# Modulation as columns, and the two gate rows multiplied in the prologue of a DiT block

## The chip, the cores and the metric

The kernel runs on one core of a Trainium2 chip. The metric is the device time in microseconds (us) of one execution. The kernel before took 2003.08 us as the median of three runs, from 2000.74 to 2003.76 us. The execution that was profiled is another one, of 2006.96 us, of which 2005.2 us lie between the first and the last instruction.

A word on names. TensorE is PE in the rows of the profile, and its weight loads are PEld. VectorE is DVE, ScalarE is ACT, GpSimd is POOL, and SyncE, which here only issues DMAs, is SP. A fp32 matmul with a full 128x128 stationary operand stands in the profile as two weight loads and two matmul records. I call one such pair a pass.

## The reference, cut to what matters

```python
x = A_x                                     # 1 x 2048 x 512, fp32
mod = silu(c) @ w_mod                       # c: 1 x 512, w_mod: 512 x 3072 -> six rows of 512
sa, ca, ga, sb, cb, gb = mod.reshape(6, 512)
h = layernorm(x) * (1 + ca) + sa
x = x + ga * attention(h, wqkv, wo)         # 32 heads of 16, softmax over 2048 keys
h = layernorm(x) * (1 + cb) + sb
x = x + gb * mixer(h, w1, w2, w3, w4)       # two token-shift / MLP stages with layernorm and gelu
```

The change is all in `mod`. Six slices of `silu(c) @ w_mod` are needed. `sa` and `ca` are used where features lie on partitions, so there each of them is a set of four columns of 128 values. `ga`, `gb`, `sb` and `cb` are used where features lie along the free axis, so each is a row of 512, the same in all 128 partitions.

## The kernel before, in words

The program has three stages. In the **prologue** x arrives in four chunks of 512 rows (`load_x`). Each chunk is normalised (`ln1`), transposed on TensorE into features on partitions (`ln1_T`, line 585), modulated with the columns `modcol`, and split into a high and a low part (`hT`). The high part is made on ScalarE (lines 590, 611, 594). The whole value comes from ScalarE or, for two of four feature blocks, from VectorE (line 597). The low part is made on GpSimd for three of four blocks (line 603). From `hT` come the first keys and queries (`qk_first`). Every product is three matmuls, high by high, high by low and low by high (lines 339, 341, 343). In **attention**, 64 units of (512 query rows, one pair of heads) follow each other. A unit has 32 score blocks on TensorE (line 1009), as many blocks for the row maximum of the unit that comes one and a half units later (line 993, reduced on VectorE in line 989), their exponentials on ScalarE (line 1005), the low half of the probabilities on GpSimd (line 1057, or ScalarE in line 127), and the product with v (lines 1080 and 1083). At its end ScalarE copies the accumulator out (line 1101), once per unit. Between the blocks of attention, TensorE is given **fill**: in the first quarter, units 0 to 15, that is the rest of k, q and v, and the modulation rows. In later quarters it is the mixer of the quarter before. The **end** is the mixer of the last quarter.

The order on each engine is fixed when the program is built. A planner (class `Sched`) keeps a made-up clock per engine. Generators are asked for their next piece of TensorE work whenever there is credit (700 ns of fill per step in the first quarter, 800 to 900 at its start). Follow-up work on the other engines is held in chains and put where the planner's clock has room. What the planner writes is executed strictly in order on every engine, whatever the true times are. All DMAs are issued by SP in the planner's order. Each of them waits for the DMA that stands eight before it.

The modulation before goes as follows.

- `load_wm(k)` loads four tiles `wm` of 128 x 1024, the first two slices of `w_mod`, two of them ahead of the first chunk of x and two behind it.
- `mod_cols` multiplies them with a broadcast `sil` as the stationary operand (line 550), eight fp32 matmuls of 512 columns. The results are rows, equal in all partitions. VectorE takes columns out of them with the identity (line 555), eight pairs of instructions.
- `mod_rows` makes the four rows within attention, from when the key group 1 is done, by `mod_gen`: for each row four chunks of 128 columns. Each chunk has one DMA of 256 KB into a staging tile `wst`, four fp32 matmuls of 128 columns (line 633) and one VectorE copy (line 637). The order is `garow`, `gbrow`, `cbrow`, and `sbrow` last, since `garow` and `sbrow` share a tile.
- `pieces_load` splits the weights of the later stages in the background. It waits for `garow` ahead of `wo` and for `gbrow` ahead of `w4`.

The first weights of v (`v_weights`) need a bound `vb`: four matmuls (line 784), then a chain on VectorE (lines 790 to 798), then a scaling on GpSimd (line 804) and a split (lines 441 and 439). With that done, the v matmuls start.

Of the kernel before, what the change touches and what calls it, by code (L numbers as in the profile page):

```python
# [310 lines left out]
def kernel(ctx, tc, A_x, A_wqkv, A_wo, B_w1, B_w2, B_w3, B_w4, c, w_mod, out):  # L311
# [23 lines left out]
    def mark(key):  # L335
        return None, 0, lambda: done.add(key)
# [9 lines left out]
    def nsq(n):  # L346
        return 0.4405 * n + 6
# [65 lines left out]
    dve.tensor_scalar(ident, iot, 0.0, None, op0=OP.is_equal)  # L413
# [95 lines left out]
    dve.tensor_tensor(sil, sil, cc, op=OP.mult)  # L509
    silb = [sil[:, k:k + 1].to_broadcast([P, P]) for k in range(KT)]  # L510
# [33 lines left out]
    def mod_cols():  # L544
        scr0 = sp.tile([P, P], F32, name="scr0")
        bs = [dbank("mr") for _ in range(2)]
        for k in range(KT):
            yield lambda: sch.now() >= arr["wm", k]
            for j in range(2):
                te.matmul(bs[j], silb[k], wm[k][:, j * D:(j + 1) * D], start=(k == 0), stop=(k == KT - 1))  # L550
                yield 4 * nsq(CH)
        for j, b in enumerate(bs):

            def diag(i, j=j, b=b):
                dve.tensor_tensor_reduce(out=scr0, in0=b[:, i * P:(i + 1) * P], in1=ident, scale=1.0, scalar=float(j),
                                         op0=OP.mult, op1=OP.add, accum_out=modcol[:, 4 * j + i:4 * j + i + 1])
                if i == 3:
                    sch.free(b)
            sch.chain(*[("D", 210, partial(diag, i)) for i in range(4)], mark(("mod", j)))

# [275 lines left out]
    def mod_rows():  # L836
        yield lambda: ("kq", 1) in done
        yield from mod_gen((2, garow, 0.0))
        done.add("garow")
        yield from mod_gen((5, gbrow, 0.0))  # L840
        done.add("gbrow")
        yield from mod_gen((4, cbrow, 1.0))
        yield lambda: all(("wo", 2 * i + c) in done for i in order["wo"] for c in range(2))
        yield from mod_gen((3, sbrow, 0.0))
        done.add("mods")
# [74 lines left out]
    for g in (mod_cols(), bounds(), ln1_T(), qk_first(hi, lo), weights_gen(), qkv_gen(0), qkv_gen(1, 2, 3, 4, 5, 6)):  # L920
        sch.add(g)
    drain(("q", 0, 0))
    for ci in range(NC):
        drain(("k", 0, ci))
        load_first(ci)
    while sch.owner or sch.back:
        sch.step()
        sch.room()
# [755 lines left out]
```

## Time and profile before

| | |
|---|---|
| median of three runs | 2003.08 us (2000.74 to 2003.76) |
| the profiled execution | 2006.96 us, span 2005.2 us |
| busy share of the span | PE 96%, DVE 82%, ACT 73%, POOL 84% |
| granted TensorE clock, mean | 0.986 |
| units 0 to 15, from the first copy of an accumulator to the seventeenth | 134.8 to 579.6 us |
| busy in that stretch (444.8 us) | PE 424.3, DVE 380.3, ACT 357.3, POOL 406.4 us |

A busy PE is not a PE at its peak: the ends of matmuls are modelled, and a record of 390 ns is followed by the next one 230 ns later. So the share of PE says little here, and starts of rows that follow each other say more. In the rows that are quoted, a bracket at the end of a row of the timeline tells how long the engine was idle before it and what ended that.

### The profile page before, as it was taken

The page shows a single profiled execution, that of the slowest core. Times are in us where ns is not written, and L with a number is a line of the kernel's source. Part 1 is how long each engine was busy: PE and PEld are TensorE (multiplying, and loading weights), DVE is VectorE, ACT ScalarE, POOL GpSimd, SP SyncE. Part 2 cuts the span into 40 slices and gives each one's busy share as a digit, 9 for nine tenths or more (in the row PEclk, how much of TensorE's full clock was granted, in tenths as well). Part 3 has the DMA queues.
Part 4 walks back from the last instruction along what each step waited for, and adds up shares of the span by engine and source line. Part 5 has one row for each costly group of instructions (what it writes and reads, how often), then busy time and mean ns, then how long its engine had stood idle before and what let it go on. Part 6 is the DMA issues. An engine that isn't in the chain of part 4 may idle for free.

```text
span 2005.2 us, 42362 instructions
## 1 busy us (share of the span) xinstructions
PE 1920.3 (96%) x14464; PEld 1146.1 (57%) x14464; DVE 1653.2 (82%) x3025; ACT 1466.3 (73%) x3072; POOL 1682.4 (84%) x1612
## 2 busy tenths in 40 slices
PE   6989999999999999999999999999999999999899
PEld 4655555555455555555455555555545555555798
DVE  7888988888898988888989888898898889892643
ACT  5375898777878887786878677787787778786443
POOL 6386999999989998888999988898898989897532
PEclk8999999999999999999999999999999999999999
DMA  5676677876543434344433333344433343333432
GB/s 186 197 205 198 199 228 218 266 231 205 174 152 111 118 132 136 97 145 138 133 106 115 107 96 111 108 136 136 152 104 97 111 136 114 111 116 111 180 146 90
DMA packets 232352, 293.24 MB, mean 146 GB/s; under 512 B 125876, under 2 KB 177076, under 8 KB 215848
## 3 DMA queue, kind: packets, MB, share of 16 engines
q1 hardware_dynamic: 232136, 290.53, 46.2%
q8 instruction: 115, 1.88, 0.4%
q14 instruction: 101, 0.83, 0.1%
HBM read 225.81 MB, written 62.91 MB: 144 GB/s over the span
## 4 chain that ended last, share of the span: by engine, by line
PE 65%; DVE 16%; ACT 8%; POOL 5%; issue 3%; DMA 2%; SPq 1%; POOLq 0%; DVEq 0%; ACTq 0%
PE mb L993 14%; DVE mx L989 9%; PE sc L1009 9%; PE pv L1083 9%; PE w L339 7%; PE w L341 6%; PE w L343 6%; PE pv L1080 4%; ACT pt L1005 4%; POOL pt L1057 3%; DVE xs L1406 1%; DVE sq L1403 1%; PE ot L1112 1%; PE mr L633 1%; SPq L106 1%
## 5 line engine op out<-in xcount | busy, mean ns | idle before, releaser
L1057 POOL TENSOR_SCALAR pt<-pt 128x1024 f16<-128x1024 uint16 x993 | 1318.9, 1367 | 120.1 <-ACT pt L1005 114.2
L989 DVE TENSOR_REDUCE mx<-mb 128x1 f32<-128x512 f32 x2048 | 1280.8, 682 | 79.2 <-PE mb L993 49.9
L1005 ACT ACTIVATE pt<-sc 128x512 int32<-128x512 f32 x2048 | 1088.6, 607 | 274.5 <-PE mb L993 214.0
L993 PE MATMUL mb<-kst,qtl 64*128 64x512 f32 x2048 | 753.2, 454 | 50.3 <-ACT pt L1005 16.5
L1009 PE MATMUL sc<-qtl,kst 64*128 64x512 f32 x2048 | 716.5, 444 | 3.8 <-DVE mx L989 1.1
L993 PEld LDWEIGHTS mb<-kst,qtl 64*128 64x128 f32 x2048 | 348.1, 193 | 257.3 <-DVE mx L989 90.1
L1009 PEld LDWEIGHTS sc<-qtl,kst 64*128 64x128 f32 x2048 | 335.8, 186 | 154.7 <-DVE mx L989 50.3
L1083 PE MATMUL pv<-pt,vst 128*32 128x512 f16 x4096 | 358.6, 397 | 0.0
L1080 PE MATMUL pv<-pt,vst 128*25 128x512 f16 (+1 forms) x2048 | 211.7, 394 | 2.0 <-POOL pt L1057 2.0
L1083 PEld LDWEIGHTS <-vst 128*32 128x32 bf16 x4096 | 91.3, 95 | 166.5 <-issue 107.9
L1413 POOL TENSOR_TENSOR g<-xs,g 128x256 fp32r<-128x256 f32 (+2 forms) x144 | 103.2, 718 | 89.1 <-ACT g L1412 86.9
L339 PE MATMUL w<-A,wr 128*128 128x256 f32 (+2 forms) x576 | 175.9, 305 | 0.8 <-ACT A L333 0.6
L341 PE MATMUL w<-A,wr 128*128 128x256 f32 (+2 forms) x576 | 170.8, 296 | 0.7 <-DVE A L329 0.7
L343 PE MATMUL w<-A,wr 128*128 128x256 f32 (+2 forms) x576 | 168.0, 292 | 0.0
L339 PEld LDWEIGHTS w<-A,wr 128*128 128x128 f32 x576 | 110.2, 191 | 35.8 <-ACT pt L1005 12.0
L339 PE MATMUL w<-wr,g 128*128 128x512 f32 x288 | 119.1, 414 | 0.6 <-ACT g L1412 0.6
L341 PEld LDWEIGHTS w<-A,wr 128*128 128x128 f32 x576 | 110.4, 192 | 13.5 <-issue 12.2
L343 PE MATMUL w<-wr,g 128*128 128x512 f32 x288 | 115.2, 400 | 0.9 <-POOL g L1413 0.9
L1520 DVE TENSOR_TENSOR x<-x,w 128x512 f32<-128x512 f32 x64 | 43.9, 686 | 85.5 <-PE w L343 85.2
L343 PEld LDWEIGHTS w<-A,wr 128*128 128x128 f32 x576 | 110.7, 192 | 5.6 <-issue 5.6
L341 PE MATMUL w<-wr,g 128*128 128x512 f32 x288 | 113.7, 395 | 0.0
L1409 ACT ACTIVATE sq<-w 128x256 f32<-128x256 f32 (+2 forms) x144 | 55.9, 388 | 72.7 <-PE w L343 69.7
(147 smaller groups left out, 2083.5 us busy)
## 6 DMA issues: line engine op xcount, KB each, us to landing
wr<-Ws SPq DMA_DIRECT2D x80, 1024.0 KB
kst<-Ks SPq DMA_DIRECT2D x189, 256.0 KB
vst<-Vs SPq DMA_DIRECT2D x252, 192.0 KB
qtl<-Qs SPq DMA_DIRECT2D x192, 64.0 KB
Vs<-vt SPq DMA_DIRECT2D x32, 384.0 KB
Ws<-wq SPq DMA_DIRECT2D x40, 256.0 KB
Ws<-wst SPq DMA_DIRECT2D x40, 256.0 KB
wst<-in_B_w_dram SPq DMA_DIRECT2D x36, 256.0 KB
```

Source lines behind the costliest of these rows:

```text
L339: te.matmul(o, lh, rh, start=first, stop=False)
L341: te.matmul(o, lh, rl, start=False, stop=False)
L343: te.matmul(o, ll, rh, start=False, stop=last)
L989: end = sch.crit("D", 605, e + PX, lambda: dve.reduce_max(mxs[u][:, j, g, c:c + 1], b, axis=AX.X))
L993: return ready, lambda: te.matmul(b, lhs, kst[u % 3][r, c * CH:(c + 1) * CH], start=True, stop=True), after
L1005: ea = sch.crit("A", 480, e + PX, lambda: act.activation(pt[s][:, j], b, AF.Exp))
L1009: return ready, lambda: te.matmul(b, kst[u % 3][r, kt * P:(kt + 1) * P], qst[u][r], start=True, stop=True), after
L1057: e_low[s] = XP["G"] + sch.crit("G", 1345, ready, lambda: pool.tensor_scalar(o, i, 0.5, 1.0, op0=OP.mult, op1=OP.mult))
L1080: te.matmul(acc[r:r + n, :], v[:, (kt + i) % 4, c - n:c].bitcast(F16), pt[s + i].bitcast(F16)[:, j, 0::2], start=False, stop=kt == NKT - 2 ...
L1083: te.matmul(acc[r:r + 32, :], v[:, kt % 4, r:r + 32], pt[s].bitcast(F16)[:, j, 1::2], start=kt == 0, stop=False, skip_group_check=True)
L1409: sch.chain(("A", cA(n), lambda: act.activation(sq, b, AF.Square)), ("D", cD(n), cube), ("A", cA(n), lambda: act.activation(sq, sq, AF.Tan ...
L1413: ("G", cG(n), lambda: pool.tensor_tensor(lo, xs, hi, op=OP.subtract)), (None, 0, end), bank=b)
```

## The change

The two slices of the columns are now multiplied the other way round. The tile of `w_mod` is the stationary operand and one column of `sil` is moved, 32 fp32 matmuls with one column each (new line 571), all into eight columns of one PSUM bank. VectorE then needs two small instructions (new line 578) in place of eight pairs. The identity is made after `sil`.

As soon as tile k of `wm` has been used, `load_wm2(k)` refills its buffer with slices 2 and 5 of `w_mod`, two DMAs of 256 KB. `mod_gates` multiplies them as rows: eight fp32 matmuls of 512 columns (new line 557), and ScalarE copies them into `garow` and `gbrow` (new line 561). `mod_rows` keeps only `cbrow` and `sbrow`. The loop at the end of the prologue waits in the planner for both gate rows.

```diff
--- before.py
+++ after.py
@@ -410,7 +410,6 @@
     psd["d"] = pp
     iot = sp.tile([P, P], I32, name="iot")
     pool.iota(iot, pattern=[[1, P]], base=0, channel_multiplier=-1)
-    dve.tensor_scalar(ident, iot, 0.0, None, op0=OP.is_equal)
 
     hT = [qp.tile([P, KT, 2, CH], F32R, name=f"hT{i}") for i in range(NC)]
     garow = sbrow
@@ -507,6 +506,7 @@
     dve.tensor_scalar(sil, sil, 1.0, None, op0=OP.add)
     dve.reciprocal(sil, sil)
     dve.tensor_tensor(sil, sil, cc, op=OP.mult)
+    dve.tensor_scalar(ident, iot, 0.0, None, op0=OP.is_equal)
     silb = [sil[:, k:k + 1].to_broadcast([P, P]) for k in range(KT)]
 
 
@@ -541,23 +541,44 @@
         sch.chain(*[("D", 670, partial(stats, t)) for t in range(TPC)], ("G", 1300, rstd), (None, 0, applies),
                   prio=2 * (ci > 1), ready=arr["x", ci])
 
-    def mod_cols():
-        scr0 = sp.tile([P, P], F32, name="scr0")
+    wm2 = {}
+
+    def load_wm2(k):
+        wm2[k] = sp.tile([P, 2 * D], F32, name="wm", tag="wm", bufs=KT)
+        for j in range(2):
+            arr["wm2", k] = sch.dma(dma.dma_start, wm2[k][:, j * D:(j + 1) * D], w_mod[k * P:(k + 1) * P, (2 + 3 * j) * D:(3 + 3 * j) * D])
+
+    def mod_gates():
+        yield lambda: len(wm2) == KT and sch.room(2)
         bs = [dbank("mr") for _ in range(2)]
         for k in range(KT):
+            yield lambda: sch.now() >= arr["wm2", k]
+            for j in range(2):
+                te.matmul(bs[j], silb[k], wm2[k][:, j * D:(j + 1) * D], start=(k == 0), stop=(k == KT - 1))
+                yield 4 * nsq(CH)
+
+        def out(d, b):
+            act.activation(d, b, AF.Copy)
+            sch.free(b)
+        for b, d, key in zip(bs, (garow, gbrow), ("garow", "gbrow")):
+            sch.chain(("A", cA(), partial(out, d, b)), mark(key), bank=b)
+
+    def mod_cols():
+        b = dbank("mr")[:, :8]
+        for k in range(KT):
             yield lambda: sch.now() >= arr["wm", k]
-            for j in range(2):
-                te.matmul(bs[j], silb[k], wm[k][:, j * D:(j + 1) * D], start=(k == 0), stop=(k == KT - 1))
-                yield 4 * nsq(CH)
-        for j, b in enumerate(bs):
-
-            def diag(i, j=j, b=b):
-                dve.tensor_tensor_reduce(out=scr0, in0=b[:, i * P:(i + 1) * P], in1=ident, scale=1.0, scalar=float(j),
-                                         op0=OP.mult, op1=OP.add, accum_out=modcol[:, 4 * j + i:4 * j + i + 1])
-                if i == 3:
-                    sch.free(b)
-            sch.chain(*[("D", 210, partial(diag, i)) for i in range(4)], mark(("mod", j)))
-
+            for i in range(8):
+                te.matmul(b[:, i:i + 1], wm[k][:, i * P:(i + 1) * P], sil[:, k:k + 1], start=(k == 0), stop=(k == KT - 1),
+                          skip_group_check=True)
+                yield 150
+            load_wm2(k)
+
+        def cols(j):
+            c = slice(4 * j, 4 * j + 4)
+            dve.tensor_scalar(modcol[:, c], b[:, c], float(j), None, op0=OP.add)
+            if j:
+                sch.free(b)
+        sch.chain(*[("D", 120, partial(cols, j)) for j in range(2)], mark(("mod", 0)), mark(("mod", 1)), prio=0, bank=b)
 
     gcol = qp.tile([P, 8], F32, name="gcol")
 
@@ -835,10 +856,6 @@
 
     def mod_rows():
         yield lambda: ("kq", 1) in done
-        yield from mod_gen((2, garow, 0.0))
-        done.add("garow")
-        yield from mod_gen((5, gbrow, 0.0))
-        done.add("gbrow")
         yield from mod_gen((4, cbrow, 1.0))
         yield lambda: all(("wo", 2 * i + c) in done for i in order["wo"] for c in range(2))
         yield from mod_gen((3, sbrow, 0.0))
@@ -917,12 +934,14 @@
         ("A", cA(), lambda i=i: act.activation(hi[:, 2 * i:2 * i + 2], w0f[:, 2 * i:2 * i + 2], AF.Copy)),
         ("D", cD(), lambda i=i: dve.tensor_tensor(lo[:, 2 * i:2 * i + 2], w0f[:, 2 * i:2 * i + 2], hi[:, 2 * i:2 * i + 2],
                                                   op=OP.subtract)))], mark("w0"), ready=arr["w0"])
-    for g in (mod_cols(), bounds(), ln1_T(), qk_first(hi, lo), weights_gen(), qkv_gen(0), qkv_gen(1, 2, 3, 4, 5, 6)):
+    for g in (mod_cols(), bounds(), mod_gates(), ln1_T(), qk_first(hi, lo), weights_gen(), qkv_gen(0), qkv_gen(1, 2, 3, 4, 5, 6)):
         sch.add(g)
     drain(("q", 0, 0))
     for ci in range(NC):
         drain(("k", 0, ci))
         load_first(ci)
+    drain("garow")
+    drain("gbrow")
     while sch.owner or sch.back:
         sch.step()
         sch.room()
```

Counted over the whole program, nothing else is added or taken away: 32 matmuls of 128 columns fewer on TensorE, 32 of one column more, eight of 512 columns as before; eight pairs less and two small ones more on VectorE, and eight copies of a chunk less; two copies more on ScalarE; eight staged DMAs of 256 KB less and eight of 256 KB more on SP. From unit 17 on, TensorE has the same number of matmuls of each kind per unit as before. What stands where changes in the first quarter, and above all at these four places.

SP at the beginning, after the loads of x. The names are `wm` for tiles of `w_mod`, `wst` for the staging tiles of the first weights of v, and `Ks` for the store of the first keys.

```order
 L106 DMA xt<-in_A_x_dram 128x4x512 x3
+L106 DMA wm<-in_w_mod_dram 128x512 x4
+L106 DMA wst_113<-in_A_wqkv_dram 128x2x256
 L106 DMA wst_114<-in_A_wqkv_dram 128x2x256
-L106 DMA wst_115<-in_A_wqkv_dram 128x2x256
+L106 DMA wm<-in_w_mod_dram 128x512 x4
 L106 DMA Ks<-qk_160 128x2x512
```

Eight DMAs of 256 KB now stand between x and the first store, four ahead of the weights of v and four behind them.

TensorE from its first instruction, before. `mr` are the modulation products, `tr` the transposes of a chunk of x, `k` the keys of the first chunk.

```order
L550 MATMUL mr<-wm,sil 128x512 x8
L585 MATMUL tr<-ident,xt 128x128 x16
L339 MATMUL k<-hT_110,wp 128x512
L341 MATMUL k<-hT_110,wp 128x512
L343 MATMUL k<-hT_110,wp 128x512
L339 MATMUL k<-hT_110,wp 128x512
L341 MATMUL k<-hT_110,wp 128x512
```

The same with the change:

```order
L571 MATMUL mr<-sil,wm 128x1 x32
L606 MATMUL tr<-ident,xt 128x128 x16
L339 MATMUL k<-hT_109,wp 128x512
L341 MATMUL k<-hT_109,wp 128x512
L343 MATMUL k<-hT_109,wp 128x512
L339 MATMUL k<-hT_109,wp 128x512
L557 MATMUL mr<-wm,sil 128x512 x4
L606 MATMUL tr<-ident,xt 128x128 x5
L557 MATMUL mr<-wm,sil 128x512 x4
L606 MATMUL tr<-ident,xt 128x128 x11
L341 MATMUL k<-hT_109,wp 128x512
```

The eight matmuls of the gates stand in the middle of the keys of the first chunk and between the transposes of the second.

VectorE where the bound of v is worked out, before. `h` is the whole value of a feature block, `hT_113` the last chunk.

```order
L795 ISA qk_158,vcol<-vb,ident 128x128
L795 ISA vcol 128x1
L795 ISA qk_158,vcol<-vb,ident 128x128
L795 ISA vcol 128x1
L797 TENSOR_SCALAR vcol<-vcol 128x2
L798 RECIPROCAL vb<-vb 128x256
L597 TENSOR_SCALAR h_156<-tr,modcol 128x512
L597 TENSOR_SCALAR h_155<-tr,modcol 128x512
L329 TENSOR_TENSOR qk_161<-k,qk_160 128x512
L603 TENSOR_TENSOR hT_113<-h_155,hT_113 128x512
```

The same with the change (the last chunk is `hT_112` there):

```order
L618 TENSOR_SCALAR h_157<-tr,modcol 128x512
L618 TENSOR_SCALAR h_155<-tr,modcol 128x512
L329 TENSOR_TENSOR qk_161<-k,qk_160 128x512
L811 TENSOR_SCALAR vb<-vb 128x256
L624 TENSOR_TENSOR hT_112<-h_155,hT_112 128x512
L816 ISA qk_158,vcol<-vb,ident 128x128
L816 ISA vcol 128x1
L816 ISA qk_158,vcol<-vb,ident 128x128
L816 ISA vcol 128x1
L818 TENSOR_SCALAR vcol<-vcol 128x2
L819 RECIPROCAL vb<-vb 128x256
```

The whole chain of `vb` has moved behind the last chunk of `h`, because the fourth matmul of `vb` now stands after the keys of the second chunk on TensorE and stood ahead of them before.

TensorE at the end of unit 0, where the first row of `mod_gen` stood and with the change still stands. Before, the chunk of `mr` belongs to `garow`:

```order
L1009 MATMUL sc<-qtl_600,kst_602 128x512 x2
L993 MATMUL mb<-kst_771,qtl_769 128x512
L633 MATMUL mr<-wst_118,sil 128x128 x4
L1112 MATMUL ot<-ident,ac 128x128 x4
L993 MATMUL mb<-kst_771,qtl_769 128x512
```

With the change it belongs to `cbrow`:

```order
L1028 MATMUL sc<-qtl_640,kst_642 128x512 x2
L1012 MATMUL mb<-kst_810,qtl_808 128x512
L654 MATMUL mr<-wst_117,sil 128x128 x4
L1131 MATMUL ot<-ident,ac 128x128 x4
L1012 MATMUL mb<-kst_810,qtl_808 128x512
```

There are eight such chunks behind this place in place of sixteen. What comes after them in the list of fill moves forward, so that the last queries end in unit 13 or 14 with 36 matmuls less left for unit 13.

## The prediction

> **What bounds the kernel now.** I read the chain of work that ended last first, from the page, then the same chain over 134 to 430 us alone, where all sixteen chunks of `mod_gen` lie.
>
> ```profile
> PE 65%; DVE 16%; ACT 8%; POOL 5%; issue 3%; DMA 2%; SPq 1%; POOLq 0%; DVEq 0%; ACTq 0%
> ...
> by line: PE mb L993 15.6%; DVE mx L989 11.7%; PE sc L1009 9.8%; PE pv L1083 9.7%; PE mr L633 5.2%; PE pv L1080 4.3%; ACT pt L1005 4.3%; issue 3.6%; DMA wst<-in_A_wqkv_dram 3.3%; DMA Vs<-vt 3.1%; PE v L341 2.5%; PE v L339 2.5%; PE k L341 2.4
> ```
>
> TensorE carries two thirds of the chain. In the second answer line 633 has 5.2% of 296 us, which is 15.4 us. Next I read what one chunk of line 633 takes, from its start to the start of what follows it:
>
> ```profile
> 135.59 1.16 PE L633 MATMUL mr<-wst,sil 128*128 128x128 f32 x8
> 136.58 0.38 PE L1112 MATMUL ot<-ident,ac 128*128 128x128 f32 x2
> ```
>
> That is 0.99 us for four matmuls, eight records. Sixteen chunks are 15.8 us, so the chain holds practically every one of them. But a chain shows one path, and another can lie close behind it. How close, the units tell. These are the copies of the accumulator, one per unit, over the first quarter and over two units that have next to no fill, and then the busy times of the same two stretches (PE, PEld, DVE, ACT, POOL):
>
> ```profile
> L1101 ACT ACTIVATE ac<-pv x17: 579/617/684, 134.8 to 579.6; 128x512 f32<-128x512 f32 x17
> L1101 ACT ACTIVATE ac<-pv x3: 628/657/684, 510.0 to 555.6; 128x512 f32<-128x512 f32 x3
> 134.80:579.60 444.80, 424.30 (x3246) 234.94 (x3246) 380.33 (x647) 357.34 (x734) 406.39 (x343) 0.98 0.70 216
> 510.00:555.60 45.60, 41.99 (x328) 18.87 (x329) 42.17 (x74) 37.54 (x78) 44.54 (x38) 0.96 0.53 168
> ```
>
> A unit without fill takes 45.6 / 2 = 22.8 us, and GpSimd is busy for 44.5 of the 45.6 us: there it is the bound. Sixteen units of the first quarter take 444.8 us, 80.0 us more than 16 x 22.8 = 364.8. This excess is what the fill costs.
>
> **What the gate rows cost in attention.** The fill on TensorE in that stretch, by groups, and the distance between two starts for matmuls of 512 and of 256 columns:
>
> ```profile
> L339 PE MATMUL q<-hT,wp 128*128 128x512 f32 x56 | 23.5, 419 | 0.0
> L339 PE MATMUL v<-wp,hT 128*128 128x256 f32 x64 | 19.2, 300 | 0.0
> L633 PE MATMUL mr<-wst,sil 128*128 128x128 f32 x128 | 19.0, 287 | 0.3 <-DMA wst<-in_w_mod_dram 0.3
> L339 PE MATMUL k<-hT,wp 128*128 128x512 f32 x32 | 13.3, 416 | 0.0
> 46.94 0.39 PE L343 MATMUL k<-hT,wp 128*128 128x512 f32 x1
> 47.16 0.40 PE L339 MATMUL k<-hT,wp 128*128 128x512 f32 x1
> 55.35 0.28 PE L339 MATMUL v<-wp,hT 128*128 128x256 f32 x1
> 55.46 0.28 PE L341 MATMUL v<-wp,hT 128*128 128x256 f32 x1
> ```
>
> Starts are 0.22 and 0.11 us apart. Each group has two sisters (lines 341 and 343), so q is 3 x 56 x 0.22 = 37.0 us, k 3 x 32 x 0.22 = 21.1, v 3 x 64 x 0.11 = 21.1, and the modulation 15.8: 95.0 us together. They cost 80.0 us of time, 0.84 us for each us of TensorE. The change takes eight of the sixteen chunks out, 8 x 0.99 = 7.9 us of TensorE. At 0.84 that is **6.7 us less**. The bounds are nothing (GpSimd, busy for 406.4 of 444.8 us, has nothing taken off it and sets the time anyway) and 7.9 us (the chain is right in full). I stay near the upper end, since the chain holds the chunks and GpSimd only 5% of the whole chain. The eight VectorE copies and the eight DMAs of 256 KB that go from this stretch I cost at nothing: VectorE is behind GpSimd by 26 us there, and SP's queue gets the same eight DMAs earlier.
>
> **The columns in the prologue.** No matmul of one column is in the trace. A fp32 matmul has two passes, so 32 have 64. Per pass the nearest rows are the chunk above, 0.99 / 8 = 0.12 us with a load hidden behind the pass before, and for a load that is not hidden at all its own duration:
>
> ```profile
> L633 PEld LDWEIGHTS mr<-wst,sil x128: 185/190/192, 135.6 to 423.4; 128*128 128x128 f32 x128
> 11.00 0.19 PEld L550 LDWEIGHTS mr<-wm,sil 128*128 128x128 f32 x1 [0.24 <-issue]
> 11.43 0.19 PEld L550 LDWEIGHTS mr<-wm,sil 128*128 128x128 f32 x1 [0.24 <-issue]
> 17.30 0.78 ACT L590 ACTIVATE h<-tr,modcol 128x512 f32<-128x512 f32 x1 [0.68 <-DVE modcol L555]
> ```
>
> So the 64 passes take between 0 and 64 x (0.19 + 0.12) = 20 us, and I take 64 x 0.12 = 7.7 us: the full load is the same tile size. The Trainium skill ("TensorE: Matmul & The Clock Gate", LDWEIGHTS) speaks against the gain that one column promises: it says that a load's time goes by its 128 columns, 128 / 1.2 = 107 ns, whatever is moved then. As an estimate from that page 64 x 0.107 = 6.8 us; the trace's 0.12 agrees, and the sum would be the same. The eight wide matmuls before are 16 passes of 0.43 us, 6.9 us: equal within a microsecond. What ScalarE waited for at 17.30 were the eight pairs of line 555; two small instructions replace them. Columns a little later and taken out faster: **0**, and if all 20 us were true, they would end some 13 us later than now, of which the gap told of next hides 6.5.
>
> **The gates in the prologue.** Eight matmuls of 512 columns are again 16 x 0.43 = 6.9 us. Here is where they go. The windows have the busy times as above, then granted clock, share of the DMA engines and GB/s:
>
> ```profile
> 15.00:20.00 5.00, 2.80 (x16) 1.86 (x16) 4.65 (x21) 4.29 (x7) 1.19 (x1) 1.00 1.04 387
> 20.00:25.00 5.00, 0.97 (x3) 0.49 (x3) 4.76 (x15) 1.37 (x3) 1.61 (x5) 0.72 0.52 177
> 25.00:30.00 5.00, 1.99 (x4) 1.01 (x4) 4.86 (x13) 1.52 (x2) 4.58 (x6) 0.50 0.01 2
> 30.00:35.00 5.00, 5.00 (x18) 4.28 (x18) 3.90 (x9) 4.50 (x7) 1.88 (x5) 0.50 0.00 0
> ...
> 20.71 0.40 PE L339 MATMUL k<-hT,wp 128*128 128x512 f32 x1
> 27.66 0.80 PE L341 MATMUL k<-hT,wp 128*128 128x512 f32 x1 [6.55 <-POOL hT L603]
> ```
>
> TensorE is idle for 6.55 us, until 27.66, and the gates stand at that place. The DMA engines move 387 GB/s until about 22.6 (half of the window from 20) and nothing from 25 to 35. The new 8 x 256 KB = 2.1 MB take 5.4 us at that rate, so the last tile lands near 28. Four gate matmuls fit into the gap, four follow after five transposes: 6.9 - 6.55 = **0.4 us later**. If the clock stays at 0.50 as it does there now, they take 13.8 us and TensorE is 7.2 us later: the upper bound. The lower bound is the rival on the clock.
>
> **The chain to the first v.** What TensorE waits for at the end of the prologue:
>
> ```profile
> 44.79 1.38 DVE L795 CUSTOM_DVE_ANT_0 qk<-vb,ident 128x128 f32<-128x128 f32 x1
> 46.32 0.76 ACT L594 ACTIVATE hT<-tr,modcol 128x512 fp32r<-128x512 f32 x1
> 47.71 1.74 DVE L798 RECIPROCAL vb<-vb 128x256 f32<-128x256 f32 x1
> 49.38 1.43 DVE L597 TENSOR_SCALAR h<-tr,modcol 128x512 f32<-128x512 f32 x2
> 51.38 3.03 POOL L804 TENSOR_TENSOR wst<-wst,vb 128x512 f32<-128x512 f32 x2
> 55.01 0.38 PE L341 MATMUL v<-wp,hT 128*128 128x256 f32 x1 [0.75 <-DVE wp L439]
> 60.88 0.96 PE L993 MATMUL mb<-kst,qtl 64*128 64x512 f32 x5 [1.35 <-DVE vr L740]
> L333 ACT ACTIVATE qk<-k 128x512 fp32r<-128x512 f32 x16 | 9.5, 596 | 19.5 <-PE k L343 19.4
> ```
>
> The chain of `vb` takes 49.38 - 44.79 = 4.6 us on VectorE and now comes after the last two `h` (1.43 us), no longer ahead of them. ScalarE ends its part of `hT` at 47.08. It gets two copies more (line 561), 1.2 us by the row of the same shape, and what is queued behind them there is `hT`, for which TensorE, VectorE and GpSimd wait: 48.3. Then 0.8 us for the last `h` and the chain of `vb`: 53.7 by its 4.6 us, or 51.5 where nothing else delays it (its two longest rows without a wait are 1.38 and 1.74; the rest is small). GpSimd's scaling began at 51.38. So the first v comes 0.1 to 2.3 us later; I take 1.1, and attention starts that much later.
>
> **The sum** for the profiled execution is 2006.96 - 6.7 + 0 + 0.4 + 1.1 = 2001.8 us, 5.2 us less. That execution lies 3.9 us above the median of the runs shown; from the median 2003.08 the same difference gives **1997.9 us**. Within this case the ends are -7.9 + 0.1 and -3.4 + 1.5 (half of 6.7 hidden): 1995.3 to 2001.2 us.
>
> **The rivals.**
>
> *The gate chunks were hidden anyway.* For it speaks GpSimd with 91% of the first quarter and 98% of the bare units, none of which goes. Against it speaks the chain. Then nothing is saved, the prologue costs its 1.5 us: 2004.6 us, no change that can be told.
>
> *The clock stays up.* The clock was 0.50 from the idle gap until 35 us, with TensorE busy for all of 30 to 35. If the gates fill the gap, and the fall does not come, then the some 7 us of work between 27.66 and 35 take half, 3.5 us less: 1994.4 us. The Trainium skill has this as a rule (same page, Part 1): the clock halves after an idle window of about 3.4 us and returns after a busy one; the trace agrees with the fall after 6.55 idle us, and by the rule the gates, which run while it is low, would bring it back earlier. Against it speaks that four matmuls of k in 15 to 22 us did not hold it, and that the gates themselves must wait for their tiles.
>
> *A new stall on the queue of DMAs: slower.* Fill moves forward in the first quarter, and with it the loads and stores of k, q and v, which stand in one order on SP with the loads of attention. The chain from 134 to 430 us holds such stalls:
>
> ```profile
> 146.07 5.80 issue
> 388.46 5.28 DMA wst<-in_A_wqkv_dram
> 393.75 4.55 DMA wst<-in_A_wqkv_dram
> ```
>
> One more of the size of the last two together, 9.8 us, at the loads of the weights or at the stores of k, gives 1997.9 + 9.8 = 2007.7 us. It makes the kernel slower from 5.2 us on. For it speaks a DMA share of 0.70 over the quarter; against it that the eight loads taken out leave the queue emptier there, and that such a stall may just as well go.
>
> **How the numbers follow.** A measurement here can tell about 0.2%, 4 us, from no change. I give the forecast 0.47, the hidden chunks 0.25, the clock 0.17 and the stall 0.11. The forecast's own range, 1995.3 to 2001.2 us, lies on both sides of 1999.1: 0.28 of it counts as faster, 0.19 as no change. The clock is faster with all 0.17. The hidden chunks are no change with 0.21, and with 0.04, where the gates cost more than 1.5 us, slower. The stall is slower with 0.09, no change with 0.02. Together faster 0.45, same 0.42, slower 0.13. The range goes from 1992, a little below the clock's time, to 2006, which takes in the hidden chunks with some of the 7.2 us and leaves out most of the stall.
>
> **What would show it.** Right: the first score-maximum matmul (60.88 now) starts 1 to 3 us later; the seventeen copies of the accumulator span 436 to 440 us in place of 444.8, with the gain in units 12 to 15, where fill has run out; from unit 17 on nothing differs. Wrong: that span is unchanged (hidden chunks), the row of the first maximum stands earlier and the clock is 1.00 over 25 to 35 us (clock), or a piece of a DMA over 5 us is new on the chain. If TensorE waits more than 3 us for `wm` between the transposes, or the one-column passes are over 0.2 us apart, the prologue was priced wrongly.

## The result and the profile after

The changed kernel takes 2013.09 us (median of 4 runs, 2012.34 to 2015.5), the kernel before 2002.84 us (2000.74 to 2003.76): a ratio of 1.0056, with a 95% interval of 1.0041 to 1.0072. It is slower by 8 to 14 us where 5 us less was predicted, and the time lies outside of the range. The kernel before, run again beside the experiments, had medians of 2001.8 to 2003.5 us and single runs from 1997 to 2013; one source of that spread is told at the end.

The chain of work that ended last, by engine and by line, on the page of the changed kernel:

```profile
PE 65%; DVE 18%; ACT 7%; POOL 5%; issue 4%; DMA 1%; SPq 0%; POOLq 0%; ACTq 0%; DVEq 0%
PE mb L1012 13%; DVE mx L1008 10%; PE sc L1028 9%; PE pv L1102 9%; PE w L339 7%; PE w L341 6%; PE w L343 6%; PE pv L1099 4%; ACT pt L1024 3%; POOL pt L1076 3%; DVE xs L1425 1%; DVE sq L1422 1%; PE ot L1131 1%; PE q L341 1%; PE q L339 1%
```

TensorE has the same 65% as before; VectorE has risen from 16 to 18%. The modulation, 1% of that list before, has left it, as it should, and the time has not fallen. Where it went, the copies of the accumulator tell (first and last start), and the busy times of the stretch between them (PE, PEld, DVE, ACT, POOL, then clock, DMA share, GB/s):

```profile
L1120 ACT ACTIVATE ac<-pv x17: 583/619/788, 142.5 to 585.7; 128x512 f32<-128x512 f32 x17
142.50:585.70 443.20, 421.33 (x3182) 228.52 (x3182) 375.20 (x639) 356.13 (x734) 406.50 (x343) 0.98 0.68 211
```

Two losses stand here. The first copy comes at 142.5 us, 134.8 before: **the prologue is 7.7 us longer**. And the seventeen copies span 443.2 us. Before, that was 444.8, but this one execution held a stall of 4 to 5 us that is not always there (below); without it the quarter took 439.5 us in a run whose attention has the same order (the columns alone, below). So **the quarter is about 4 us longer, with 64 matmul records fewer** (3182, before 3246). After the seventeenth copy every unit lasts as long as before to within 0.3 us, but for two of 0.4 and 0.7 us.

In the prologue two waits stand out. VectorE, then TensorE, then GpSimd, each from the timeline of its engine (start, duration, instruction, and in brackets the idle time ahead of it and its releaser):

```profile
12.34 0.18 DVE L351 BATCH_NORM_AGGREGATE mv<-st 128x2 f32<-128x6 f32 x1
19.39 0.23 DVE L578 TENSOR_SCALAR modcol<-mr 128x4 f32<-128x4 f32 x2 [6.87 <-PE mr L571]
19.53 0.99 DVE L527 TENSOR_SCALAR xt<-xt,mv,rs 128x512 f32<-128x512 f32 x2
```

```profile
5.54 13.81 PE L571 MATMUL mr<-sil,wm 128*128 128x1 f32 x64 [5.54 <-DVE sil L508]
20.13 3.92 PE L606 MATMUL tr<-ident,xt 128*128 128x128 f32 x16 [0.78 <-DVE xt L527]
57.05 0.40 PE L343 MATMUL k<-hT,wp 128*128 128x512 f32 x1
61.11 0.58 PE L339 MATMUL v<-wp,hT 128*128 128x256 f32 x1 [3.67 <-ACT wp L440]
69.59 0.74 PE L1012 MATMUL mb<-kst,qtl 64*128 64x512 f32 x4 [1.30 <-DVE vr L761]
```

```profile
59.13 2.50 POOL L825 TENSOR_TENSOR wst<-wst,vb 128x512 f32<-128x512 f32 x2 [3.80 <-DVE vb L819]
```

The 64 one-column passes take 13.81 us, 0.216 us each. VectorE's small instruction on the columns stands ahead of the normalisation of `x` and of twelve more statistics, and VectorE stands still for 6.87 us with all of that behind it. At the other end, GpSimd gets `vb` at 59.13 us, 51.38 before, and the first `v` starts at 61.11 us, 53.88 before. The row of before:

```profile
53.88 0.38 PE L339 MATMUL v<-wp,hT 128*128 128x256 f32 x1 [0.28 <-ACT wp L441]
```

### The profile page after: what moved, and what is told of

Read it like the earlier page. It is cut to its first block, busy times and chain, and to the rows that moved or that the text cites. A ratio compares the mean times of both kernels' runs of the same rounds, so it can differ in the third digit from the quotient of the medians.

```text
span 2011.8 us, 42318 instructions
## 1 busy us (share of the span) xinstructions
PE 1930.4 (96%) x14464; PEld 1155.6 (57%) x14464; DVE 1645.1 (82%) x3003; ACT 1465.8 (73%) x3074; POOL 1680.3 (84%) x1612
## 4 chain that ended last, share of the span: by engine, by line
PE 65%; DVE 18%; ACT 7%; POOL 5%; issue 4%; DMA 1%; SPq 0%; POOLq 0%; ACTq 0%; DVEq 0%
PE mb L1012 13%; DVE mx L1008 10%; PE sc L1028 9%; PE pv L1102 9%; PE w L339 7%; PE w L341 6%; PE w L343 6%; PE pv L1099 4%; ACT pt L1024 3%; POOL pt L1076 3%; DVE xs L1425 1%; DVE sq L1422 1%; PE ot L1131 1%; PE q L341 1%; PE q L339 1%
## 5 line engine op out<-in xcount | busy, mean ns | idle before, releaser
L1099 PE MATMUL pv<-pt,vst 128*17 128x512 f16 (+1 forms) x2048 | 211.9, 393 | 2.4 <-POOL pt L1076 2.4
```

The costliest lines, as they stand in the source:

```text
L1099: te.matmul(acc[r:r + n, :], v[:, (kt + i) % 4, c - n:c].bitcast(F16), pt[s + i].bitcast(F16)[:, j, 0::2], start=False, stop=kt == NKT - 2 ...
```

## The experiments

The text ahead of each result tells what was expected of that run. What is called the first copy is the first copy of the accumulator, and the quarter is the time from there to the seventeenth.

**The kernel before, a second time.**

> The kernel before, unchanged, profiled a second time. Its first profiled execution, 2006.96 us, lies 4.1 us above the median of its runs. If that execution held a stall that is rare (the 9.8 us of DMA for wst on the chain at 388 to 398 us), this one ends near 2002 us and units 8 to 10 are together about 4 us shorter. If the stall is always there, the units end as in the first profile to within 1 us.

It took 2006.07 us, and its copies go from 134.5 to 579.6 us. Neither theory held: units 8 to 10 were as in the first profile, but unit 1 took 32.2 us in place of 36.5, and unit 13 took 35.9 in place of 32.3. The piece of DMA at 388 us was thus no loss of the first execution alone. A stall had moved from one unit to another.

**The halves of the change, one at a time.** Columns alone:

```diff
-            for j in range(2):
-                te.matmul(bs[j], silb[k], wm[k][:, j * D:(j + 1) * D], ...)
+            for i in range(8):
+                te.matmul(b[:, i:i + 1], wm[k][:, i * P:(i + 1) * P], sil[:, k:k + 1], ...)
```

> The columns of the modulation by 32 one-column matmuls, as in the change; the two gate rows stay in attention, as before. Theory (the columns make the prologue late: 64 passes of 0.216 us at half clock, 13.8 us, with VectorE held behind them): the first accumulator copy is 5 to 7 us later than before, attention is as before, 2008 to 2010 us. Rival (the gates in the prologue make it late, the columns don't): first copy within 2 us, 2003 us.

Gates alone:

```diff
+            load_wm2(k)
...
-    for g in (mod_cols(), bounds(), ln1_T(), ...
+    for g in (mod_cols(), bounds(), mod_gates(), ln1_T(), ...
-        yield from mod_gen((2, garow, 0.0))
-        yield from mod_gen((5, gbrow, 0.0))
```

> The columns as before (eight wide matmuls, eight products with the identity); the gate rows in the prologue, as in the change. Theory (columns are the prologue's loss, and what the gate chunks gave in units 2 and 3 is lost again in units 8 to 14): first copy 1 to 2 us later, then 8 us gained by unit 7 and given back by unit 16: 2003 to 2006 us. Rival (the gates are the prologue's loss): first copy 5 to 7 us later, 2008 to 2011 us. Second rival (my prediction's attention term holds and only columns spoil it): 1997 to 1998 us.

The columns alone took 2004.92 us (ratio 1.0008, 0.9993 to 1.0023), the gates alone 2009.55 us (1.0035, 1.0019 to 1.0052). The copies of the two, in this order:

```profile
L1121 ACT ACTIVATE ac<-pv x17: 578/607/697, 138.9 to 578.4; 128x512 f32<-128x512 f32 x17
```

```profile
L1122 ACT ACTIVATE ac<-pv x17: 597/616/792, 138.4 to 583.6; 128x512 f32<-128x512 f32 x17
```

Against 134.8 us the first copy is 4.1 us later with the columns and 3.6 us later with the gates; together 7.7, the change's loss. That it fits to the tenth is luck: with the order of before the first copy came at 134.8, 134.5 and 133.6 us (the first profile, e1 and e9). No theory held in full: the columns cost less than the 5 to 7 us expected, the gates more than 1 to 2, and with the gates alone units 1 to 7 gained under 2 us (193.4 us in place of 195.1 with the columns alone) where 8 were expected. The columns' run leaves attention in its old order: its quarter is 439.5 us, and I take this as the quarter of before without a large stall. The gates' run has the change's order, and its units 8 to 11 last 30.5, 36.3, 30.1 and 34.0 us, in the change 30.4, 36.3, 30.1 and 34.0: that stretch is no accident of one execution.

**What the chunks cost in attention, with a new plan.**

```diff
-        yield from mod_gen((2, garow, 0.0))
         done.add("garow")
-        yield from mod_gen((5, gbrow, 0.0))
         done.add("gbrow")
```

> The kernel before without the two gate rows: they are set to ones and not computed, so eight chunks and their DMAs are gone and nothing is put in their place. It measures what the chunks cost in attention. Prediction's term: 6.7 us less, 1996 us. Hidden chunks: 2003 us. Theory from the two traces (work that moves forward in units 8 to 11 costs more there than it gives back in units 12 to 14, which GpSimd bounds): 8 us less until unit 7, of which 5 to 8 are lost by unit 16, 2000 to 2005 us.

```diff
-        yield from mod_gen((2, garow, 0.0))
+        yield from mod_gen((2, garow, 0.0), (2, garow, 0.0))
...
-        yield from mod_gen((5, gbrow, 0.0))
+        yield from mod_gen((5, gbrow, 0.0), (5, gbrow, 0.0))
```

> The kernel before with the eight chunks of the gate rows computed twice in attention, 24 chunks in place of 16 (same results; eight loads, eight times four matmuls and eight VectorE copies more). Prediction's price, 0.84 us for each us of TensorE: 6.7 us more, 2009 us. Theory (the chunks lie in time that other engines set, and move the rest of the fill about at will): within 3 us of before, 2000 to 2006 us.

Without the chunks (the two rows are set to ones and not computed) the kernel took 2005.7 us (1.0012, 0.9993 to 1.003), so taking work away gained nothing; with the chunks twice 2019.78 us (1.0065, 1.0045 to 1.0086), 13 us more by the ratio where the prediction's price gave 6.7 and the theory 3 at most. Taking chunks away gains nothing and adding them costs twice their price: one price for a us of TensorE cannot explain both.

**Is it GpSimd, or the budget of fill?**

```diff
-                      ("G", cG(), lambda f=f, t=t, w=w: pool.tensor_tensor(t, f, w, op=OP.subtract)),
+                      (None, 0, lambda: None),
```

> The kernel before without GpSimd's subtractions that make the low parts of most weights of the second half (the group wst<-wst,wq on GpSimd, 40 instructions of 1.05 us, 42.0 us, in units 1 to 14); the parts are stored unsplit, so this part of the computation is left out. TensorE's work is the same. Theory (GpSimd and the engines beside it set the first quarter's time, not TensorE's fill): 20 to 40 us less, the seventeen copies of the accumulator span 400 to 425 us. Rival (TensorE sets it, 0.84 us for each us of fill): span within 5 us of 440, time within 5 us of before.

```diff
-SC0 = (32, 900.0, 700.0)
+SC0 = (32, 900.0, 640.0)
```

> The kernel before without the gate rows (set to ones, not computed) and with the planner's budget of fill lowered from 700 to 640 ns for a step of attention, so that the fill left over is spread as in before. Theory (e4_no_gate_rows gained nothing because the planner put other fill into the freed places, and bunched it): 3 to 7 us less than e4_no_gate_rows, 1998 to 2003 us. Rival (GpSimd's and ScalarE's work sets the time however TensorE's fill is spread): within 2 us of e4_no_gate_rows, 2004 to 2008 us.

The second edit stands on top of e4's. With 42 us of GpSimd's subtractions gone, the only execution of the kernel took 2023.1 us, 17 us more than the profiled run of e1: units 7 to 9 went from 28.4, 25.0 and 34.1 us to 38.2, 37.1 and 40.2. GpSimd was relieved by less than was taken out, since the planner gave it 12 instructions more of line 1057, work that ScalarE did before: its busy time in the quarter fell from 407.0 to 384.4 us. Both theories fell. The lower budget took 2005.86 us (1.0002, 0.9985 to 1.002), the rival's time: at 640 ns the size of the budget is not it. Both runs had again the order of the fill as a second thing that had altered.

**The same order, and the same work.** The next two tell work and order apart. In the first every instruction of before keeps its place; the matmuls of the two rows are not issued, and the eight copies of their results only set ones. The planner still counts the matmuls:

```diff
-                    te.matmul(b, silb[k], f3[:, k], start=(k == 0), stop=(k == KT - 1))
+                    if j not in (2, 5):
+                        te.matmul(b, silb[k], f3[:, k], start=(k == 0), stop=(k == KT - 1))
                     yield 2 * nsq(P)
```

> The kernel before with every instruction in its old order on every engine, but the 32 matmuls of the eight chunks of the gate rows left out (their eight VectorE copies are memsets of the same rows; loads stay). The gate rows are not computed. It is the price of the chunks on TensorE with no other instruction moved. Prediction's term: 6.7 us less, 1996 us, and the quarter from the first to the seventeenth accumulator copy 433 us in place of 439.5. Rival (hidden: other engines end these stretches anyway): within 2 us of before, 2001 to 2004 us. If it is 6.7 us less, the loss of e4_no_gate_rows (3 us more than before with the same matmuls gone) is the new order of the rest.

In the second the instructions are the same, and one number of the planner alters their order:

```diff
-CFILL = 200.0
+CFILL = 180.0
```

> The kernel before with one number of the planner altered (20 ns less charged for each visit to the fill): the same instructions, but the fill in another order, in units 1 to 7 nearly that of the change (k of both blocks in unit 1, then v by 36, 36, 48, 36 matmuls a unit). Theory (an order that was fitted to this work is lost with any new plan): 3 to 8 us more than before, 2006 to 2011 us. Rival (order matters little, the work decides): within 2 us of before.

The first took 1999.66 us, the kernel before beside it 2003.52 (0.998, 0.9965 to 0.9996): **3.9 us less for 7.9 us of TensorE**. The second took 2015.16 us (1.0051, 1.0032 to 1.007): **10 us more for no work at all**. Their copies:

```profile
L1105 ACT ACTIVATE ac<-pv x17: 581/620/696, 133.6 to 570.2; 128x512 f32<-128x512 f32 x17
```

```profile
L1101 ACT ACTIVATE ac<-pv x17: 597/603/653, 133.5 to 584.8; 128x512 f32<-128x512 f32 x17
```

436.6 and 451.3 us, against 439.5. Not all of the 451.3 need be order: this execution held one long subtraction on VectorE, of the kind told at the end.

```profile
377.81 4.19 DVE L890 TENSOR_TENSOR wst<-wst,wq 128x512 fp32r<-128x512 f32 x1
```

But with 4 us off, 447 us are still 8 more than 439.5, and the four executions lie between 2013.5 and 2016.6 us. The order of the fill weighs more than eight chunks of it.

**The columns: what is their loss?** The planner counts 150 ns for a one-column matmul. Told what two passes take, it puts VectorE's instruction elsewhere:

```diff
-                yield 150
+                yield 430
```

> The change with one number altered: the planner is told 430 ns, not 150 ns, for each one-column matmul, which is what two passes of 0.216 us take on the chip. VectorE's instruction on the columns then stands behind the normalisation of the first x and behind statistics, and VectorE is not held for 6.9 us at 12.5 us. Theory (the columns' cost in the prologue is VectorE held behind a matmul that the planner believed done): first copy 3 to 4 us earlier than in the change, 2008 to 2010 us. Rival (the columns' cost is the late transposes on TensorE, which start at 20 us either way): first copy as in the change, 2012 to 2014 us.

And with the clock raised ahead of them:

```diff
+        for _ in range(5):
+            te.matmul(b0, zz[:, :P], zz, start=True, stop=True)
```

> The change with five wide matmuls on zeros ahead of the columns, so that TensorE is busy from about 1.6 us on; every other instruction keeps its order. Theory (the one-column passes take 0.216 us because the clock is at half): granted clock 1.00 before 8 us, passes 0.11 us apart, the columns end near 13 us in place of 19.35, first copy 3 to 6 us earlier than in the change, 2007 to 2010 us. Rival (0.216 us is what such a pass takes, or the clock falls again under one-column passes): columns end after 18 us, 2012 to 2014 us.

With the true cost VectorE no longer waits for the columns. Its timeline, and the copies:

```profile
12.42 0.18 DVE L351 BATCH_NORM_AGGREGATE mv<-st 128x2 f32<-128x6 f32 x1
14.10 1.00 DVE L527 TENSOR_SCALAR xt<-xt,mv,rs 128x512 f32<-128x512 f32 x2 [1.50 <-POOL rs L355]
```

```profile
L1120 ACT ACTIVATE ac<-pv x17: 585/627/783, 137.8 to 581.7; 128x512 f32<-128x512 f32 x17
```

The columns are no faster (they end at 19.36 us), the last of the statistics starts at 28.4 us in place of 33.8, and the first copy starts at 137.8 us, 4.7 us earlier than in the change and 3.0 later than before, which leaves about what the gates cost alone. So the columns' loss was VectorE, held behind an instruction that the planner believed due. The time was still 2011.41 us (1.004, 1.002 to 1.0059): attention had got another order once more, with a unit 9 of 42.2 us in the profiled execution, which at 2005.84 us was the fastest of ten. The warmed columns took 2013.6 us (1.0044, 1.0027 to 1.0061), the rival's time. They end at 17.46 us, not near 13, and the first copy comes 2.0 us earlier than in the change. What they show of the clock stands at the end.

```profile
L1126 ACT ACTIVATE ac<-pv x17: 597/617/761, 140.5 to 589.0; 128x512 f32<-128x512 f32 x17
```

**The change, with the order kept.** If the order is the loss, the same change must do without it. In these three the planner goes on counting the eight chunks in attention, though nothing is issued for them, and the gates' matmuls are put by hand behind the first four matmuls of `k` (e13 and e14 with the columns of before, e15 with those of the change):

```diff
+                n += 1
+                if not gated and nm == "k" and ci == 0 and n == 4:
+                    gates()
...
-            e = sch.dma(dma.dma_start, f3[:, :, o:o + x.shape[2]], x)
+            e = sch.dma((lambda o, i: None) if skip else dma.dma_start, f3[:, :, o:o + x.shape[2]], x)
```

> The whole computation. Every instruction of attention in its order of before; the eight chunks' matmuls, loads and copies are gone. The columns are as before (wide). The gate rows' eight matmuls stand behind the first four matmuls of k, in the idle gap of 6.55 us, and their tiles are loaded ahead of the last x. Theory (the new order was the change's loss in attention, and the gap takes the gates when their tiles are there in time): first copy within 1 us of before, quarter as in the run with the same order, 1998 to 2000 us. Rival (the gates cost the prologue 3 us wherever they stand): first copy 3 us later, 2002 to 2003 us.

> As e13, but the gate rows' tiles are loaded behind the last x, as in the change. Theory (the gates wait for their tiles, which end near 28 us, and hold the k behind them): first copy 2 to 4 us later than in e13, 2001 to 2004 us. Rival (the gap hides the wait): as e13.

> The whole change (one-column matmuls, gate rows in the prologue, loads behind the last x), with every instruction of attention in its order of before, and VectorE's instruction on the columns where the products with the identity stood. Theory (new order and VectorE held are the change's losses): quarter from first to seventeenth copy about 436 us, first copy 3 to 5 us later than before, 2001 to 2004 us, 9 us less than the change. Rival (the work itself is the loss, in whatever order): 2010 us or more.

They took 1999.53 us (0.9994, 0.997 to 1.0019), 1999.05 us (0.9988, 0.9974 to 1.0001) and 2000.43 us (0.9994, 0.9982 to 1.0007), the kernel before 2001.78. e13 came out as its theory had it in time and first copy; e14 and e15 were 2.0 and 0.6 us faster than the ranges expected, and e15's first copy was 2.0 us later than before where 3 to 5 were expected. The copies of the three, in this order (the profiled execution of e13 held three long subtractions, told at the end):

```profile
L1128 ACT ACTIVATE ac<-pv x17: 580/610/685, 135.5 to 581.8; 128x512 f32<-128x512 f32 x17
```

```profile
L1127 ACT ACTIVATE ac<-pv x17: 587/617/677, 137.4 to 574.4; 128x512 f32<-128x512 f32 x17
```

```profile
L1131 ACT ACTIVATE ac<-pv x17: 578/615/683, 136.8 to 573.9; 128x512 f32<-128x512 f32 x17
```

The whole change in the old order is 12.7 us faster than the change as it was made, by the medians; by the two profiles the first copy is 5.7 us earlier and the quarter 6.1 us shorter (437.1 against 443.2). It does not beat the kernel before by more than can be told. The early loads do what the gap promised: in e13 the gates' matmuls fill the gap, and `k` goes on at 27.67 us, 27.66 before:

```profile
20.95 7.03 PE L690 MATMUL mr<-wm,sil 128*128 128x512 f32 x16
27.67 0.54 PE L341 MATMUL k<-hT,wp 128*128 128x512 f32 x1
```

In e14, with the loads behind `x`, `k` goes on at 31.18 us and the first copy is 1.9 us later than in e13. One attempt to keep the order failed:

> A version with the whole computation: columns as before (wide), the gate rows in the prologue but last in priority behind the transposes and the first k and q, and in attention the planner still charged for the eight chunks that are no longer there (no matmul, no load, no copy). Theory (order is what the change lost): the fill's order is again not that of before, so 2000 to 2008 us; only if the charge kept the order would it be 1997 us. Rival (what lies in the prologue decides): first copy as before, 1996 to 1998 us.

It took 2023.89 us (1.0104, 1.0082 to 1.0126). The planner counted the chunks, but the prologue had moved its clocks, and the order in attention was new all the same: units 7 and 9 took 42.5 and 40.9 us, 14 and 7 more than before, in an execution 8 us above the median. The time lies above both of its theories.

**Where the order loses.** The change and e15 issue the same work in the quarter. Units 1 to 7, 8 to 11 and 12 to 14 of the change, then of e15:

```profile
142.50:333.40 190.90, 182.73 (x1441) 101.09 (x1442) 166.32 (x289) 165.94 (x350) 176.72 (x154) 0.98 0.71 211
333.40:464.20 130.80, 123.50 (x852) 70.58 (x852) 98.78 (x165) 93.50 (x189) 114.58 (x94) 0.97 0.74 238
464.20:539.20 75.00, 70.61 (x535) 34.85 (x533) 66.71 (x113) 60.38 (x123) 72.10 (x61) 1.00 0.58 181
```

```profile
136.80:328.60 191.80, 182.37 (x1454) 103.01 (x1454) 167.61 (x290) 162.35 (x344) 180.35 (x157) 0.99 0.69 208
328.60:444.80 116.20, 112.22 (x814) 62.45 (x813) 94.73 (x161) 92.93 (x185) 106.13 (x87) 0.99 0.74 239
444.80:526.70 81.90, 79.21 (x564) 40.70 (x564) 67.91 (x116) 64.54 (x130) 78.47 (x66) 0.96 0.64 205
```

Units 1 to 7 are equal to within 1 us. In units 8 to 11 the change has 852 records of TensorE against 814, and 94 instructions of GpSimd against 87; it takes 14.6 us longer and gets back 6.9 us in units 12 to 14. Part of this is work that has moved: the 8.5 us more of GpSimd's busy time stand against 3.6 less in units 1 to 7, which are only 0.9 us shorter for it, and 6.4 less in units 12 to 14, which give back the 6.9. The clock does not tell the two apart: the trace has 13.6 us at half clock in the quarter of each. Which instructions of the new order cost the rest is not settled: no single wait of TensorE in unit 8, the first of the four, is longer than 2.6 us.

## Why the prediction was wrong, step by step

- **What bounds the kernel.** That the chain holds nearly all sixteen chunks was right, and so was the excess of 80 us over the bare units, though 4 to 5 us of it were the stall. The step from there is not confirmed: 0.84 us of time for each us of TensorE is a mean over fill of all kinds, and I used it as the price of one kind. With all else in place eight chunks cost 3.9 us, 0.5 for each us; the interval, 0.8 to 7.0 us, does not exclude the 6.7.
- **The gate rows in attention, -6.7 us.** This is the step that failed. The term held the rest of the order still, and the change does not. I had noted that the work behind the chunks moves forward, and used it only to say in which units the gain would show. Measured, order and chunks together are about +4 us on the quarter: roughly -3 for the chunks (436.6 against 439.5) and +6 for the order (443.2 against 437.1, one execution each; e3 and e11, with the change's order in attention, had 445.2 and 448.4). The same planner makes +10 us of a change that alters no work.
- **Columns, 0.** The pass was priced at 0.12 us, which is right at full clock, and took 0.216. My own sign of a wrong price, passes over 0.2 us apart, came true. But even so the late columns did not cost the time directly, as e7 shows: the price was in VectorE's order, which I had not read at this place. Measured +4.1 us on the first copy.
- **Gates in the prologue, +0.4, and the chain to the first v, +1.1.** Together 3.6 us by the gates alone. The gap does take the gates, as said, but only if their tiles are there: with the loads behind `x` they wait for the first tile, and `v` comes 2.75 us later (53.88 before), where the text had 0.1 to 2.3. In the change itself it comes 7.2 us later: the last `h` is done at 55.1 us where I had 49.1. The chain of `vb` did take 2.5 us (56.57 to 59.06) and not 4.6, but the 51.5 us of the text do not follow from the two rows it names, which give 52.2. The timeline of TensorE in e3:
```profile
22.72 8.83 PE L557 MATMUL mr<-wm,sil 128*128 128x512 f32 x16 [4.55 <-DMA wm<-in_w_mod_dram]
56.63 0.38 PE L339 MATMUL v<-wp,hT 128*128 128x256 f32 x1 [4.10 <-ACT wp L441]
```

- **The rivals.** The hidden chunks came nearest in their number for attention and had the wrong reason: the chunks are not hidden, they are paid back by the order. The clock behaved in e13 as that rival said, 1.00 from 20 to 30 us and 0.80 over 30 to 35 us with the gates in the gap, and gained nothing: its first copy is 0.7 us later than before. That rival tied the fall to 6.55 idle us, but its own row, 0.72 over 20 to 25 us, puts it near 22.2 us, one us into the gap and behind a stretch with few matmuls. The stall on the DMA queue was on the right side, and the first maximum at 69.59 us in place of 60.88 was outside of all that I named.
- **The chances.** Slower had 0.13, 0.09 of it for a stall on one queue. The chance that a new plan as such loses time was not in the list, though the planner's part was told ahead of the prediction.

## What to carry to other kernels

Where a planner writes one fixed order for several engines from modelled costs, a change of any item makes a new order for everything behind it, and here the order alone cost about 6 us in attention in the change and 10 us in a change without work, against 4 us that the item was worth. Which places of an order lose was not found here. So price the item with the order held (leave its instructions out, but let the planner count them), price the order by itself with a change that alters no work, and only then judge the change; a change that is right can be kept by keeping the order. And an instruction that a planner believes due holds everything behind it on its engine: whenever a new kind of operation comes in, look first at what stands behind its consumer.

## What the runs showed of the hardware

**One-column matmuls do not keep TensorE's clock up.** After the wide matmuls of e11 the columns started at full clock. Its windows (busy times, granted clock, DMA share, GB/s):

```profile
8.00:12.70 4.70, 4.70 (x44) 4.68 (x42) 3.15 (x8) 0.00 (x0) 0.64 (x4) 0.99 1.08 375
12.70:17.50 4.80, 4.76 (x23) 4.67 (x22) 0.00 (x1) 2.67 (x4) 1.49 (x4) 0.50 1.04 380
```

Until 12.62 us the passes are 0.111 us apart, and from there on 0.214: the clock fell 4.6 us into an unbroken row of them, with TensorE 100% busy by the profile. In the change the row started at half clock and never rose in 13.8 us, and the same row in e2, e7 and e15 had the same 0.21 us between passes. Wide matmuls at that place did raise it: before, the passes of 512 columns start at 5.62 us, are 0.85 us apart at first and 0.43 us from 8.86 us on. (The clock shown as 1.00 in the first us of a profile is what stands there until the first record; the distance of the passes tells.) The Trainium skill ("TensorE: Matmul & The Clock Gate", Part 1) says that the first 3.4 us or so run slow whatever is issued, and all behind them fast; for passes of one column these runs show otherwise.

**One subtraction on VectorE can last 6 us.** This is the stall that moves from execution to execution. In the first profile of before, VectorE and then GpSimd:

```profile
145.67 6.28 DVE L439 TENSOR_TENSOR wp<-wst,wp 128x512 fp32r<-128x512 f32 x1
151.87 1.27 DVE L989 TENSOR_REDUCE mx<-mb 128x1 f32<-128x512 f32 x2
```

```profile
145.74 0.46 POOL L1123 TENSOR_TENSOR osb<-sm,rc 128x128 f32<-128x128 f32 x1
146.10 0.26 POOL L1042 TENSOR_TENSOR nm<-mf,nm 128x8 fp32r<-128x8 f32 x1
146.27 3.93 POOL L1057 TENSOR_SCALAR pt<-pt 128x1024 f16<-128x1024 uint16 x3
150.08 1.31 POOL L891 TENSOR_TENSOR wst<-wst,wq 128x512 fp32r<-128x512 f32 x1
```

The other thirteen of line 439 in this execution take 0.68 to 1.67 us. The same instruction of the same order in e9 took 1.78 us, beside the same row of GpSimd:

```profile
146.84 1.78 DVE L439 TENSOR_TENSOR wp<-wst,wp 128x512 fp32r<-128x512 f32 x1
```

```profile
145.52 4.29 POOL L1061 TENSOR_SCALAR pt<-pt 128x1024 f16<-128x1024 uint16 x3
149.74 1.28 POOL L895 TENSOR_TENSOR wst<-wst,wq 128x512 fp32r<-128x512 f32 x1
```

In the first profile it ends 0.6 us after GpSimd's row of six instructions without a gap. The chain put that time down to "issue 5.80", which the prediction had counted among the stalls of the DMA queue. The Trainium skill ("SBUF — State Buffer", Who interferes with whom) says that a VectorE instruction with two inputs in SBUF contends with a GpSimd instruction that reads SBUF, and that the port pair they share is an exclusive lock. By that the loser waits for one instruction; here the subtraction would have waited for a row of six. But a row without a gap is not enough: in e9 the subtraction began in the middle of one and was done at 148.62 us, while GpSimd's three instructions took 4.29 us in place of 3.93. So the cause is argued from these traces and not shown, and what decides who waits stays open. In one execution of e13, 11 us above its median, three such subtractions lasted 2.9, 4.4 and 6.4 us.
